# Four more on-chip buffers, and a new choice of buffer for every step, in a fused attention and gated-convolution kernel

## The chip, the cores and the metric

The kernel runs on one core of a Trainium2 chip. The core has five engines with a queue of instructions each: PE (TensorE, matrix products; its weight loads are listed apart as PEld), DVE (VectorE), ACT (ScalarE), POOL (GpSimd) and SP (SyncE, which here only issues DMA transfers). Each engine takes its own queue strictly in order; between engines, semaphores make an instruction wait. The metric is the device time of one execution in microseconds (us), the median of several runs.

## What is computed

The batch is 8, the heads 8, the sequence 576 tokens, the head size 64; channels of all heads together are 512. All is float32 (the weights come in as 64-bit floats and are narrowed on the chip).

```python
kv  = einsum('bhsd,bhse->bhde', k, v)          # 64 x 64 for each batch element and head
out = einsum('bhsd,bhde->bhse', q, kv)
x   = out / sqrt(mean(out * out, -1) + 1e-6) * g_norm   # then (B, S, H*D)
gate = sigmoid(sum_k conv_w[k] * x shifted by 4 - k tokens)   # causal, 5 taps, per channel
val  = x @ w_val                                # 512 x 512
return (gate * val) @ w_out                     # 512 x 512
```

## The kernel before

**Steps and their order.** The kernel is a list of 1,238 small steps, written out in a string `PLAN` (L19) and run one by one by the loop at L863. A step is a name, its arguments and, after an `@`, the numbers of the buffers that it takes: `fast_keep 0 3 0 @ 2` takes buffer 2 of its kind. A step puts one or a few instructions into the queue of one engine. There is no other scheduler: each engine does its steps in the order of the list. Semaphore waits are put in by the layer that records the instructions: an instruction waits for earlier instructions of the list on other engines which wrote what it reads, or which still use the buffer that it overwrites. A bank of PSUM (where PE writes its results) is treated as one buffer, also where two steps use different halves of it.

**Buffers.** `ROOMS` (L274) sets how many buffers a kind has and how large they are; `new` (L282) takes the next number off the list that the step brought along. The kinds in question are `ot` (output chunks of 128 tokens x 512 channels, 3 buffers), `gate` (3), `x` (normalised chunks of 128 tokens, 2), `sq` (squares of a chunk, 2), and the 8 banks of PSUM. `w64` (3 buffers) holds staged weights at first and sums of tokens later; `xs` (4) holds sums of x.

**One batch element, b = 0 to 7.** `load_half` and `load_q` bring k, v and q (SP). `kv_product` (PE, L475) and `kv_copy` (ACT) make kv. `turn_q` (DVE) turns q. `raw_pair` and `raw_tail` (PE, L549) make q times kv for two chunks, and the last half chunk, of 128 tokens. For each chunk, `square` (ACT, L583), `sums` (DVE, L592) and `powers` (POOL, L600) make the root, and `normalise` (ACT, L619: one instruction for each head, 8 for a chunk) writes an `x` buffer. x is then turned, for whole chunks from b = 2 on by `turn_blocks` (DVE, L644) and `move_blocks` (DMAs of SP and POOL, L652), else by `turn_x` (PE, L631) and `keep_x` (ACT, L638). The gate of one of four groups of channels is `gate_start` (ACT, L663), four `gate_tap` (DVE, L669) and `gate_end` (ACT sigmoid, L676) in a `gate` buffer; `gated` (DVE, L694) multiplies it into the values.

**The two large products.** From b = 2 on, x times w_val is made with seven products of blocks in place of eight: `x_sums` (DVE, L715) makes sums, `val_fast` (PE, L730; n = 0 to 6) the products, `val_keep` (copies by ACT, L739 to L751, and additions by DVE, L737) brings them together. The first two elements use `val_product` (PE, L681) and `keep_val` (ACT, L690). The output product is made likewise, for pairs of elements i and pairs of chunks p: `token_sums` (DVE, L799), `fast_product i p n` (PE, L821), `fast_keep i p n`. Bank a collects products n = 0, 2, 4 and 6 one after the other; another bank has b (n = 3) in its first half and c (n = 1, 5) in its second:

```python
if n == 0:   nc.scalar.copy(out=first[:, LOW], in_=a)       # L833, takes an ot buffer
elif n == 1: nc.scalar.copy(out=second[:, HIGH], in_=c)     # L835, takes an ot buffer
elif n == 2: nc.scalar.copy(out=first[:, HIGH], in_=a)      # L837
elif n == 4: add(second[:, HIGH], a)                        # L831, DVE
elif n == 5: add(first[:], both halves of b, c)             # L831, DVE
else:        copy(out=second[:, LOW], in_=a)                # L844
```

So product 2 may not be added to bank a before copy 0 has read it, and product 4 not before copy 2. `out_product` (PE, L768) and `keep_out` (ACT, L776) do the half chunks. `store` (SP, L853) writes a chunk out in four transfers; `store_last` shares the last two chunks between SP and ACT. An `ot` buffer is free for new data when the four transfers of the chunk before have landed.

Of the kernel before, what the change touches and what calls it, by code (L numbers as in the profile page):

```python
# [25 lines left out]
narrow_weight cw 0 1; sort_q 0 4; narrow_weight cw 0 2; narrow_weight cw 0 3; narrow_weight wval 1 0 @ 1;
stage_weight wout 0 @ 1; narrow_weight cw 0 4; narrow_weight wval 1 1; narrow_weight cw 0 6 @ 1;
narrow_weight cw 0 7; narrow_weight wval 1 2; turn_cw @ 1; kv_product 0 0; keep_cw; load_half v 1 0;
narrow_weight wval 1 5 @ 1; narrow_weight wval 1 3; narrow_weight wval 1 6 @ 0; start_warm 1 256 @ 1;
kv_copy 0 1; kv_copy 0 0; load_half k 1 0; narrow_weight wval 0 0 @ 0; raw_whole 0 4 @ 3;  # L30
# [5 lines left out]
narrow_weight wval 3 1; turn_q_rows 1 2 @ 6; sums 0 1; square 0 0 @ 0; powers 0 2; normalise 0 3 @ 0;
turn_q_rows 1 1 @ 7; narrow_weight wval 3 2; narrow_weight wval 3 6 @ 2; sort_q 1 2 @ 0; turn_q_rows 1 0 @ 2;
sums 0 0; sort_q 1 1; narrow_weight wval 3 3; turn_x 0 3 @ 6; narrow_weight wval 0 4; turn_q_rows 1 3 @ 7;
powers 0 1; normalise 0 4 @ 1; keep_x 0 3; normalise 0 2 @ 0; sort_q 1 4; turn_x 0 4 @ 3;
narrow_weight wval 3 4; load_q 2 0; turn_x 0 2 @ 4; keep_x 0 4; narrow_weight wval 2 5 @ 1;  # L40
kv_product 1 1 @ 6 5; narrow_weight wval 0 7; keep_x 0 2; narrow_weight wval 2 0 @ 0; val_product 0 0 1 @ 4;
narrow_weight wval 3 7; narrow_weight wval 2 1; halo 0; normalise 0 0 @ 0; narrow_weight wval 2 2;
narrow_weight wout 0 5 @ 2; normalise 0 1 @ 1; narrow_weight wval 2 3; load_q 2 2; turn_x 0 0 @ 0;
narrow_weight wout 0 6 @ 0; turn_x 0 1 @ 1; narrow_weight wval 2 4; keep_x 0 0; val_product 0 1 1 @ 3;
keep_val 0 0 1; narrow_weight wval 2 6 @ 2; keep_x 0 1; narrow_weight wval 2 7; gate_start 0 0 @ 0;
# [10 lines left out]
square 1 1 @ 0; val_product 0 2 0 @ 4; turn_q 2 2 @ 0; keep_x 1 4; gate_tap 0 3 1; powers 1 2;
normalise 1 3 @ 1; load_q 3 1; gate_tap 0 2 3; kv_product 2 1 @ 2 3; val_sums 1; square 1 0 @ 1; sums 1 1;
val_product 0 3 0 @ 7; normalise 1 2 @ 0; narrow_weight wout 1 4; powers 1 1; gate_tap 0 3 0;
stage_weight wout 3 @ 0; keep_val 0 2 0; sums 1 0; narrow_weight wout 0 3; turn_x 1 2 @ 1; turn_q 2 0;
turn_x 1 3 @ 4; powers 1 0; keep_x 1 2; kv_product 2 0; val_sums 3; keep_x 1 3; load_q 2 3; keep_val 0 3 0;  # L60
narrow_weight wout 0 4; normalise 1 1 @ 1; val_product 1 1 1 @ 4; narrow_weight wout 2 5 @ 2; halo 1;
narrow_weight wout 0 7; narrow_weight wout 1 7; gate_end 0 1; narrow_weight wout 2 6 @ 0;
val_product 1 3 1 @ 7; normalise 1 0 @ 0; turn_q 2 1; narrow_weight wout 3 5 @ 2; load_q 3 0;
narrow_weight wout 2 0 @ 0; kv_copy 2 0; keep_val 1 1 1; narrow_weight wout 3 6 @ 1; turn_x 1 0 @ 0;
narrow_weight wout 2 1; narrow_weight wout 3 0 @ 1; val_product 1 2 1 @ 4; keep_x 1 0; gate_tap 0 2 2;
narrow_weight wout 2 2; load_half v 3 0 @ 0; turn_q 2 3; load_half k 3 1 @ 0; kv_copy 2 1;
narrow_weight wout 2 3; load_half k 3 0 @ 0; gate_tap 0 2 1; turn_x 1 1 @ 3; load_q 3 2; gate_end 0 3;
raw_pair 2 3 @ 2 0; narrow_weight wout 2 4; keep_val 1 2 1; keep_x 1 1; gate_tap 0 2 0; raw_pair 2 1 @ 4 6;
square 2 2 @ 1; gated 0 1; load_half v 3 1 @ 0; gate_end 0 2; val_product 1 0 1 @ 3; gated 0 3; keep_val 1 3 1;
gate_start 1 1 @ 2; sums 2 2 @ 0 1; square 2 1 @ 0; gated 0 2; powers 2 2; square 2 0 @ 1; turn_q 3 1 @ 1;  # L70
val_product 1 0 0 @ 7; narrow_weight wout 3 1; sums 2 1; narrow_weight wout 3 2; sums 2 0; powers 2 1;
narrow_weight wout 3 3; val_product 1 3 0 @ 1; gate_tap 1 1 3; keep_val 1 0 0; narrow_weight wout 3 4;
square 2 3 @ 1; normalise 2 2 @ 1; narrow_weight wout 3 7; powers 2 0; val_product 1 1 0 @ 7; sums 2 3;
weight_sums 0; keep_val 1 0 1; normalise 2 1 @ 0; token_sums 0 0 0 @ 0; powers 2 3; val_product 1 2 0 @ 3;
turn_blocks 2 2; narrow_weight wout 2 7; normalise 2 0 @ 1; gate_tap 1 1 2; fast_product 0 1 0 @ 5;
turn_blocks 2 1; keep_val 1 3 0; weight_sums 2; keep_val 1 2 0; kv_product 3 1 @ 6 4; keep_val 1 1 0;
# [5 lines left out]
fast_product 0 0 4; move_blocks 2 1; gate_start 1 3 @ 1; sums 2 4; fast_product 0 1 2; weight_sums 3;
move_blocks 2 2; fast_keep 0 0 5; raw_pair 3 3 @ 6 4; move_blocks 2 0; fast_keep 0 1 2; fast_keep 0 0 4;
gate_tap 1 0 3; raw_pair 3 1 @ 1 7; store 0 0; square 3 2 @ 1; gated 1 1; powers 2 4; square 3 3 @ 0;
fast_product 0 0 6; gate_tap 1 3 3; gate_start 1 2 @ 2; move_blocks 2 3; sums 3 2 @ 1 0; fast_product 0 1 4;
fast_keep 0 0 6; sums 3 3; square 3 1 @ 1; fast_product 0 1 1 @ 3; gate_tap 1 0 2; normalise 2 4 @ 1;
# [811 lines left out]
```

## Time and profile before

| | |
|---|---|
| median of 3 runs | 306.62 us (306.56 to 308.01) |
| the profiled execution's own time | 308.16 us |
| its span, first to last instruction | 306.4 us |
| granted TensorE clock, mean | 0.997 |
| PE busy / DVE / ACT / POOL | 294.8 / 272.5 / 194.1 / 111.5 us |
| HBM read and written | 39.21 and 9.44 MB |

The profile is one execution. Its page lists busy time of each engine, the span in 40 slices, DMA queues, the chain of work that ended last and the costliest groups of instructions; the trace behind it answers further questions by window, tile or line. A row of a timeline gives the start, the length, the engine, the line and the operation with the tile written and the tiles read, merged where equal ones follow each other. In a list of waits, "A <- B: 5.8, 5, 1.9" means that A's engine sat idle before A for 5.8 us in total, 5 times, at most 1.9 us, until B released it. Buffer numbers are left out of the tiles' names: `bank` is any bank, `w` any `w64` buffer. [...] A DMA is told as `out_dram<-ot`, what it writes and reads.

### The profile page before, as it was taken

The numbers are of one execution on the slowest core, as the hardware profiler recorded it, in microseconds if no ns is written. First come the engines' busy times: TensorE is split into PE (matmuls) and PEld (weight loads), VectorE is DVE, ScalarE is ACT, GpSimd is POOL, SyncE is SP. The second block draws the span as 40 slices with busy tenths as digits, with TensorE's granted clock in tenths as the row PEclk, the third lists the DMA queues.
The fourth block names the chain that finished last, engine by engine and source line by source line (L and its number), as shares of the span: only waits on it lengthen the run. The fifth ranks groups of instructions, "written<-read, shape, count | busy, mean of one in ns | idle before, by whom it ended". The sixth has DMA issues, their size and how long they took to land.

```text
span 306.4 us, 8926 instructions
## 1 busy us (share of the span) xinstructions
PE 294.8 (96%) x3407; PEld 231.4 (76%) x3407; DVE 272.5 (89%) x486; ACT 194.1 (63%) x598; POOL 111.5 (36%) x127
## 2 busy tenths in 40 slices
...
GB/s 271 380 375 396 232 274 151 179 324 53 101 159 301 294 194 198 258 183 213 175 253 258 157 118 241 214 182 150 166 73 34 2 155 63 96 34 71 100 71 103
DMA packets 32074, 55.53 MB, mean 181 GB/s; under 512 B 6166, under 2 KB 14358, under 8 KB 32032
## 3 DMA queue, kind: packets, MB, share of 16 engines
...
q0 software_dynamic: 1632, 3.17, 4.4%
...
q8 instruction: 27, 0.44, 0.6%
q14 instruction: 15, 0.12, 0.1%
HBM read 39.21 MB, written 9.44 MB: 159 GB/s over the span
## 4 chain that ended last, share of the span: by engine, by line
PE 63%; DVE 11%; DMA 9%; ACT 7%; SPq 5%; issue 3%; POOL 1%; ACTq 0%; DVEq 0%; POOLq 0%
PE bank L821 24%; PE bank L730 16%; PE bank L681 7%; DMA out_dram<-ot 6%; PE bank L549 5%; PE bank L475 5%; PE bank L768 5%; SPq L853 4%; DVE gate L669 3%; DMA qs<-in_q_dram 2%; ACT x L619 2%; ACT gate L676 1%; DVE qT L532 1%; DVE ss L592 1%; PE bank L631 1%
## 5 line engine op out<-in xcount | busy, mean ns | idle before, releaser
L669 DVE SCALAR_TENSOR_TENSOR gate<-xT,cwT,gate 128x576 f32<-128x576 f32 x128 | 101.0, 807 | 1.3 <-ACT gate L663 1.0
L600 POOL TENSOR_TENSOR rt<-ss,mhalf 128x8 f32<-128x8 f32 (+3 forms) x38 | 68.6, 1816 | 68.6 <-DVE ss L592 68.3
L619 ACT ACTIVATE x<-bank,rt 128x64 f32<-128x64 f32 x252 | 55.8, 376 | 3.8 <-POOL rt L600 3.5
L652 POOL DMA_DIRECT2D xT<-y x48 | 26.7, 560 | 71.7 <-DVE w L799 25.5
L821 PE MATMUL bank<-wsum,w 128*128 128x256 f32 x192 | 49.2, 386 | 2.1 <-ACT ot L833 1.4
L821 PEld LDWEIGHTS bank<-wsum,w 128*128 128x128 f32 x192 | 35.3, 190 | 10.1 <-ACT ot L833 3.2
L730 PE MATMUL bank<-xs,vsum 128*128 128x288 f32 x144 | 38.7, 408 | 0.0
L681 PE MATMUL bank<-xT,wval 128*128 128x288 f32 x128 | 33.1, 411 | 0.0
L821 PE MATMUL bank<-wout,gv 128*128 128x256 f32 x128 | 32.6, 383 | 0.1
L730 PEld LDWEIGHTS bank<-xs,vsum 128*128 128x128 f32 x144 | 27.1, 190 | 7.4 <-issue 0.4
L681 PEld LDWEIGHTS bank<-xT,wval 128*128 128x128 f32 x128 | 23.6, 190 | 6.1
L831 DVE TENSOR_TENSOR ot<-bank,ot 128x512 f32<-128x512 f32 (+1 forms) x32 | 17.6, 551 | 11.8 <-ACT ot L837 5.7
L821 PEld LDWEIGHTS bank<-wout,gv 128*128 128x128 f32 x128 | 23.9, 190 | 4.3 <-ACT ot L835 0.5
L592 DVE TENSOR_REDUCE ss<-sq 128x8 f32<-128x520 f32 (+1 forms) x40 | 25.0, 632 | 2.2 <-ACT sq L583 2.0
L676 ACT ACTIVATE gate<-gate 128x576 f32<-128x576 f32 x32 | 22.2, 706 | 7.2 <-DVE gate L669 7.1
L730 PE MATMUL bank<-xT,wval 128*128 128x288 f32 x96 | 26.2, 408 | 0.2 <-issue 0.2
L583 ACT ACTIVATE sq<-bank 128x256 f32<-128x256 f32 (+1 forms) x70 | 21.3, 382 | 7.1 <-PE bank L549 7.0
L663 ACT ACTIVATE gate<-xT,cwT 128x576 f32<-128x576 f32 x32 | 25.1, 797 | 1.1 <-DVE gv L694 0.9
L694 DVE TENSOR_TENSOR gv<-gv,gate 128x576 f32<-128x576 f32 x32 | 23.8, 755 | 1.6 <-ACT gate L676 1.3
L730 PEld LDWEIGHTS bank<-xT,wval 128*128 128x128 f32 x96 | 17.9, 190 | 5.0 <-issue 0.3
L549 PEld LDWEIGHTS bank<-kv,qT 64*64 64x64 f32 x1008 | 16.6, 135 | 5.3 <-issue 3.7
L475 PEld LDWEIGHTS bank<-v,k 64*64 64x64 f32 x1008 | 16.4, 135 | 4.9 <-issue 2.8
...
## 6 DMA issues: line engine op xcount, KB each, us to landing
...
```

The source lines that it names most:

```text
L475: nc.tensor.matmul(st["kvps", b][s][r * D:(r + 1) * D, i], st["k", b, i][rows, r, cols], st["v", b, i][rows, r, cols], start=(j == 0), sto ...
L549: nc.tensor.matmul(st["raw", b, c][r][cols, to * D:(to + 1) * D], st["qT", b][rows, hp, first:first + D], kvs[b % 2][rows, hp, :], start=T ...
L592: nc.vector.reduce_sum(out=st["ss", b][:, FIRST[c]:FIRST[c] + n], in_=st["sq", b, c][:, 0:n], axis=AX.X)
L600: nc.gpsimd.tensor_tensor(out=st["rt", b][:, which], in0=st["ss", b][:, which], in1=mhalf[:, which], op=ALU.pow)
L619: nc.scalar.activation(out=x[:, to * D:(to + 1) * D], in_=raw[:, h * D:(h + 1) * D], func=AF.Copy, scale=root[:, to:to + 1])
L652: (nc.sync if i % 2 else nc.gpsimd).dma_start(out=xTs[b % 2][i * TB:(i + 1) * TB, :, first:first + P], in_=y[a * TB:(a + 1) * TB, i])
L663: nc.scalar.activation(out=gate[:], in_=xTs[b % 2][:, jt, HALO:SX], func=AF.Copy, scale=cwT[:, K - 1, jt:jt + 1])
L669: nc.vector.scalar_tensor_tensor(out=gate[:], in0=xTs[b % 2][:, jt, tap * TB:tap * TB + S], scalar=cwT[:, tap, jt:jt + 1], in1=gate[:], op ...
L676: nc.scalar.activation(out=gate[:], in_=gate[:], func=AF.Sigmoid)
L681: nc.tensor.matmul(val[:], wval[:, kc, jt * P:(jt + 1) * P], xTs[b % 2][:, kc, HALO + n * SV:HALO + (n + 1) * SV], start=(kc == 0), stop=( ...
L730: nc.tensor.matmul(st[bank, "val", b, mj][:], weights_[:, k], tokens()[:, k], start=(n in (0, 1, 3) and k == 0), stop=(k == NK // 2 - 1), ...
L821: nc.tensor.matmul(st[bank, i, p], tokens()[:, k], weights_[:, k], start=(n < 2 and k == 0), stop=(k == NK // 2 - 1), skip_group_check=True)
```

## The change

`ot` gets a fourth buffer, `gate` a fourth, `x` a third and `sq` a third; the number of all other buffers stays. The numbers behind the `@` are chosen anew for 474 steps: each step takes the buffer of its kind, banks included, that has been free for the longest time. The list's steps are the same 1,238. Many shift by a few places in the list, but the order on each engine, and on each queue, is the same, except that the third `sq` buffer is cleared at the start by one more memset of DVE (L324). One pair changes sides across engines: `fast_keep 2 2 1` (ACT) now stands ahead of `fast_product 2 2 3` (PE) in the list, both of which use the bank of b and c.

```diff
-    ROOMS = {"w64": (3, 1024), "ot": (3, 512), "wexp": (2, 512), "gate": (3, 576), "xs": (4, 576), "x": (2,
+    ROOMS = {"w64": (3, 1024), "ot": (4, 512), "wexp": (2, 512), "gate": (4, 576), "xs": (4, 576), "x": (3,
...
-             36), "rt": (2, 36), "sq": (2, 520)}
+             36), "rt": (2, 36), "sq": (3, 520)}
```

Of the plan, the lines that the prediction speaks of:

```diff
-keep_val 0 2 1; gate_tap 0 1 0; keep_val 0 1 0; powers 1 3; gate_start 0 2 @ 0; sums 1 2; turn_x 1 4 @ 2;
+powers 1 3; keep_val 0 1 0; gate_start 0 2 @ 3; sums 1 2; turn_x 1 4 @ 0; square 1 1 @ 0; turn_q 2 2 @ 0;
...
-val_fast 6 1 0 @ 1; powers 7 2; fast_keep 1 2 5; gate_tap 5 1 2; fast_product 1 2 6; fast_keep 1 3 0 @ 0;
+fast_keep 1 3 0 @ 3; powers 7 2; val_fast 6 1 0 @ 0; fast_keep 1 2 5; gate_tap 5 1 2; store 1 4;
...
-fast_product 2 2 4; gate_start 6 0 @ 0; gate_tap 6 3 1; fast_keep 2 3 0 @ 1; fast_product 2 2 3;
-gate_tap 6 0 3; move_blocks 7 2; fast_keep 2 2 1 @ 0; token_sums 2 1 3; fast_product 2 3 2; powers 7 4;
+fast_keep 2 2 1 @ 1; gate_tap 6 0 3; move_blocks 7 2; fast_product 2 2 3; token_sums 2 1 3; fast_product 2 3 2;
```

More of the change, by code (lines that the diff above doesn't have):

```diff
@@ L26 @@
[L26 to L30, printed above, removed]
@@ L36 @@
[L36 to L40, printed above, removed]
@@ L41 @@
[L41 to L45, printed above, removed]
@@ L56 @@
[L56 to L60, printed above, removed]
@@ L61 @@
[L61 to L76, printed above, removed]
@@ L82 @@
[L82 to L86, printed above, removed]
@@ L87 @@
-powers 3 3; load_half v 4 0 @ 0; fast_product 0 1 3; gate_tap 1 2 3; square 3 0 @ 0; gate_tap 1 0 1;
-turn_x 2 4 @ 0; load_half k 4 1 @ 0; val_fast 2 0 3 @ 2; load_q 4 0; fast_keep 0 1 1 @ 1; powers 3 2; sums 3 0;
-normalise 3 3 @ 1; fast_product 0 1 5; fast_keep 0 1 4; gate_tap 1 2 2; fast_product 0 1 6; gate_tap 1 3 2;
-keep_x 2 4; load_q 4 1; powers 3 0; normalise 3 2 @ 0; val_fast 2 0 0 @ 0; fast_keep 0 1 5; x_sums 2 0 @ 0;
-val_fast 2 1 0 @ 3; fast_keep 0 1 6; sums 3 1; halo 2; val_keep 2 0 0; val_fast 2 0 1 @ 5; x_sums 2 1 @ 1;
@@ L107 @@
-fast_product 0 3 1 @ 6; gate_tap 2 1 2; normalise 3 4 @ 1; fast_product 0 2 5; sums 4 2 @ 1 1; gate_end 2 3;
-gate_tap 2 1 1; fast_product 0 2 6; powers 4 2; fast_keep 0 2 5; turn_x 3 4 @ 2; load_q 5 0;
-raw_pair 4 1 @ 0 7; fast_keep 0 2 6; sums 4 3; keep_x 3 4; gated 2 3; val_fast 3 0 0 @ 2; powers 4 3;
-square 4 0 @ 0; gate_tap 2 1 0; val_fast 3 0 3 @ 1; sums 4 0; val_keep 3 0 0; square 4 1 @ 1; x_sums 3 0 @ 0;
-load_half v 5 1 @ 0; halo 3; val_fast 3 1 0 @ 5; store 0 4; val_keep 3 0 3; x_sums 3 2 @ 1; val_fast 3 1 3 @ 1;
@@ L147 @@
-gated 3 1; powers 5 4; move_blocks 5 3; fast_product 1 1 6; val_keep 4 0 6; gate_tap 4 0 1;
-out_product 1 8 @ 5; val_keep 4 1 3; normalise 5 4 @ 1; gate_tap 4 3 1; gate_start 4 2 @ 2; gate_tap 4 0 0;
-kv_copy 6 0; gate_tap 4 3 0; turn_q 6 0 @ 1; gate_end 4 3; gate_tap 4 2 3; turn_x 5 4 @ 0; load_q 6 3;
-val_fast 5 1 0 @ 4; keep_x 5 4; gated 4 3; halo 5; val_fast 5 0 0 @ 0; x_sums 5 0 @ 3; gate_start 4 1 @ 0;
-turn_q 6 2; load_half k 7 1 @ 0; fast_keep 1 1 6; val_fast 5 1 1 @ 6; load_half v 7 1 @ 0; val_keep 5 0 0;
@@ L177 @@
-fast_product 1 2 4; gate_tap 5 1 3; square 7 2 @ 0; sums 7 3 @ 1 0; val_fast 6 0 0 @ 3; keep_x 6 4;
-fast_keep 1 2 1 @ 2; gate_tap 5 3 0; fast_product 1 2 5; sums 7 2; val_keep 6 0 0; fast_keep 1 2 4;
-val_fast 6 1 0 @ 1; powers 7 2; fast_keep 1 2 5; gate_tap 5 1 2; fast_product 1 2 6; fast_keep 1 3 0 @ 0;
-store 1 4; val_keep 6 1 0; gate_end 5 3; x_sums 6 0 @ 3; val_fast 6 1 3 @ 2; powers 7 3; normalise 7 2 @ 1;
-x_sums 6 1 @ 0; fast_product 1 3 2; gated 5 3; val_fast 6 0 2; gate_tap 5 1 1; fast_keep 1 3 2; halo 6;
@@ L197 @@
-move_blocks 7 0; val_keep 6 0 5; fast_product 2 2 5; gate_tap 6 2 2; fast_keep 2 3 2; gate_tap 6 0 2;
-fast_product 2 3 4; normalise 7 4 @ 1; gate_tap 6 2 1; val_fast 6 0 6; gate_tap 6 2 0; turn_x 7 4 @ 4;
-fast_product 2 3 1 @ 6; val_keep 6 0 6; gate_tap 6 3 0; keep_x 7 4; fast_product 2 3 3; halo 7;
-fast_keep 2 2 4; gate_tap 6 0 1; fast_product 2 2 6; gate_tap 6 0 0; val_fast 7 0 0 @ 4; x_sums 7 0 @ 1;
-gate_end 6 0; fast_keep 2 2 5; val_fast 7 1 0 @ 3; fast_keep 2 2 6; gate_end 6 2; x_sums 7 1 @ 3; store 2 4;
@@ L222 @@
-fast_keep 3 2 2; fast_keep 3 2 5; fast_product 3 2 4; store 3 4; fast_product 3 3 0 @ 0; fast_keep 3 2 4;
-fast_product 3 2 6; fast_keep 3 3 0 @ 1; fast_product 3 3 2; fast_product 3 3 3; fast_keep 3 3 2;
-fast_keep 3 2 6; fast_product 3 3 4; store 3 5; fast_keep 3 3 1 @ 2; fast_product 3 3 5; fast_keep 3 3 4;
+stage_weight cw 0 @ 0; turn_q_rows 0 4 @ 1; turn_q_rows 0 2 @ 2; turn_q_rows 0 1 @ 3; turn_q_rows 0 3 @ 4;
+sort_q 0 1 @ 0; turn_q_rows 0 0 @ 5; start_warm 3 256 @ 6; sort_q 0 0; load_q_rows 1 0; stage_weight wval 3;
@@ new lines @@
+turn_x 0 4 @ 4; load_q 2 0; turn_x 0 2 @ 6; narrow_weight wval 2 5 @ 0; keep_x 0 4; kv_product 1 1 @ 7 3;
+narrow_weight wval 0 7; keep_x 0 2; narrow_weight wval 2 0 @ 0; narrow_weight wval 3 7; narrow_weight wval 2 1;
+val_product 0 0 1 @ 4; halo 0; normalise 0 0 @ 0; narrow_weight wval 2 2; load_q 2 2;
+narrow_weight wout 0 5 @ 2; normalise 0 1 @ 1; narrow_weight wval 2 3; narrow_weight wout 0 6 @ 1;
+turn_x 0 0 @ 6; turn_x 0 1 @ 5; narrow_weight wval 2 4; keep_x 0 0; val_product 0 1 1 @ 1;
+narrow_weight wval 2 6 @ 3; keep_val 0 0 1; keep_x 0 1; narrow_weight wval 2 7; gate_start 0 0 @ 0;
@@ new lines @@
+val_product 0 2 0 @ 1; keep_x 1 4; powers 1 2; normalise 1 3 @ 0; gate_tap 0 3 1; load_q 3 1; gate_tap 0 2 3;
+kv_product 2 1 @ 6 3; val_sums 1; square 1 0 @ 2; sums 1 1; normalise 1 2 @ 1; val_product 0 3 0 @ 0;
+narrow_weight wout 1 4; powers 1 1; gate_tap 0 3 0; stage_weight wout 3 @ 2; keep_val 0 2 0;
+narrow_weight wout 0 3; sums 1 0; turn_x 1 2 @ 5; turn_q 2 0; powers 1 0; turn_x 1 3 @ 7; keep_x 1 2;
+kv_product 2 0; val_sums 3; load_q 2 3; keep_x 1 3; narrow_weight wout 0 4; keep_val 0 3 0; normalise 1 1 @ 2;
@@ new lines @@
+val_product 1 1 1 @ 1; narrow_weight wout 2 5 @ 3; halo 1; narrow_weight wout 0 7; narrow_weight wout 1 7;
+gate_end 0 1; narrow_weight wout 2 6 @ 2; normalise 1 0 @ 1; val_product 1 3 1 @ 5; turn_q 2 1;
+narrow_weight wout 3 5 @ 1; load_q 3 0; narrow_weight wout 2 0 @ 1; kv_copy 2 0; narrow_weight wout 3 6 @ 0;
+keep_val 1 1 1; narrow_weight wout 2 1; turn_x 1 0 @ 7; narrow_weight wout 3 0 @ 0; val_product 1 2 1 @ 0;
+gate_tap 0 2 2; keep_x 1 0; load_half v 3 0 @ 0; narrow_weight wout 2 2; turn_q 2 3; load_half k 3 1 @ 0;
@@ new lines @@
+kv_copy 2 1; load_half k 3 0 @ 0; narrow_weight wout 2 3; gate_tap 0 2 1; load_q 3 2; turn_x 1 1 @ 2;
+gate_end 0 3; narrow_weight wout 2 4; raw_pair 2 3 @ 6 4; keep_val 1 2 1; gate_tap 0 2 0; keep_x 1 1;
+raw_pair 2 1 @ 1 7; gated 0 1; square 2 2 @ 1; load_half v 3 1 @ 0; gate_end 0 2; gated 0 3;
+val_product 1 0 1 @ 3; keep_val 1 3 1; sums 2 2 @ 0 0; gate_start 1 1 @ 0; gated 0 2; square 2 1 @ 0;
+powers 2 2; square 2 0 @ 2; turn_q 3 1 @ 1; val_product 1 0 0 @ 0; narrow_weight wout 3 1; sums 2 1;
@@ new lines @@
+kv_product 3 1 @ 7 1; keep_val 1 1 0; turn_q 3 0; turn_q 3 2; load_q 3 3; fast_product 0 0 1 @ 2;
+gate_tap 1 1 1; fast_product 0 0 3; token_sums 0 0 1; fast_keep 0 0 1 @ 3; normalise 2 3 @ 0;
+token_sums 0 0 2 @ 0; fast_product 0 0 0 @ 0; weight_sums 1; kv_product 3 0; gate_tap 1 1 0;
+fast_keep 0 0 0 @ 1; gate_start 1 0 @ 2; token_sums 0 0 3; raw_tail 2 @ 4 5; kv_copy 3 1; fast_product 0 0 2;
+kv_copy 3 0; turn_blocks 2 3; gate_end 1 1; turn_blocks 2 0; fast_product 0 0 5; fast_keep 0 0 2; turn_q 3 3;
@@ new lines @@
+fast_keep 0 1 0 @ 0; move_blocks 2 1; square 2 4 @ 0; fast_product 0 0 4; gate_start 1 3 @ 1; sums 2 4;
+move_blocks 2 2; weight_sums 3; fast_product 0 1 2; fast_keep 0 0 5; move_blocks 2 0; raw_pair 3 3 @ 6 1;
+fast_keep 0 0 4; fast_keep 0 1 2; gate_tap 1 0 3; store 0 0; raw_pair 3 1 @ 2 7; powers 2 4; gated 1 1;
+square 3 2 @ 2; square 3 3 @ 1; gate_tap 1 3 3; fast_product 0 0 6; gate_start 1 2 @ 3; move_blocks 2 3;
+sums 3 2 @ 1 1; fast_product 0 1 4; sums 3 3; fast_keep 0 0 6; square 3 1 @ 0; gate_tap 1 0 2;
@@ new lines @@
+fast_product 0 1 1 @ 0; powers 3 3; normalise 2 4 @ 1; load_half v 4 0 @ 0; gate_tap 1 2 3; fast_product 0 1 3;
+square 3 0 @ 2; load_half k 4 1 @ 0; gate_tap 1 0 1; fast_keep 0 1 1 @ 2; turn_x 2 4 @ 4; load_q 4 0;
+val_fast 2 0 3 @ 5; powers 3 2; normalise 3 3 @ 0; sums 3 0; fast_keep 0 1 4; fast_product 0 1 5;
+gate_tap 1 2 2; keep_x 2 4; load_q 4 1; fast_product 0 1 6; gate_tap 1 3 2; powers 3 0; normalise 3 2 @ 2;
+fast_keep 0 1 5; val_fast 2 0 0 @ 4; x_sums 2 0 @ 0; fast_keep 0 1 6; val_fast 2 1 0 @ 0; sums 3 1; halo 2;
@@ new lines @@
+square 4 3 @ 2; fast_keep 0 2 4; gate_tap 2 1 2; square 4 2 @ 0; fast_product 0 3 1 @ 2; normalise 3 4 @ 0;
+sums 4 2 @ 0 0; fast_product 0 2 5; gate_end 2 3; gate_tap 2 1 1; powers 4 2; load_q 5 1; fast_product 0 2 6;
+fast_keep 0 2 5; sums 4 3; turn_x 3 4 @ 0; fast_keep 0 2 6; raw_pair 4 1 @ 6 1; keep_x 3 4; gated 2 3;
+powers 4 3; gate_tap 2 1 0; square 4 0 @ 1; load_q 5 0; sums 4 0; val_fast 3 0 0 @ 7; val_fast 3 0 3 @ 3;
+val_keep 3 0 0; square 4 1 @ 0; val_fast 3 1 0 @ 0; x_sums 3 0 @ 0; halo 3; load_half v 5 1 @ 0;
@@ new lines @@
+val_keep 3 0 3; val_keep 3 1 0; store 0 4; x_sums 3 2 @ 2; val_fast 3 1 3 @ 3; normalise 4 2 @ 1;
+x_sums 3 1 @ 1; powers 4 0; fast_product 0 3 3; gate_tap 2 0 2; normalise 4 3 @ 2; val_fast 3 0 2;
+val_keep 3 1 3; load_q 5 2; sums 4 1; val_fast 3 0 1 @ 3; gate_tap 2 0 1; powers 4 1; gate_tap 2 0 0;
+val_fast 3 1 2; turn_blocks 4 3; gate_end 2 0; val_fast 3 1 1 @ 4; x_sums 3 3 @ 3; val_keep 3 0 1;
+gate_start 2 2 @ 1; val_fast 3 0 5; gated 2 0; val_keep 3 1 1; store 0 5; val_keep 3 0 2; gate_tap 2 2 3;
@@ new lines @@
+fast_keep 0 3 6; fast_keep 0 3 5; raw_pair 5 3 @ 3 1; store 0 7; fast_keep 1 0 2; powers 4 4; gate_tap 3 0 3;
+raw_pair 5 1 @ 7 5; token_sums 1 0 3 @ 1; square 5 3 @ 1; move_blocks 4 0; gate_tap 3 0 2; normalise 4 4 @ 1;
+fast_product 1 1 1 @ 2; sums 5 3 @ 1 1; square 5 0 @ 0; move_blocks 4 1; fast_product 1 0 1 @ 0;
+gate_tap 3 3 1; square 5 2 @ 2; powers 5 3; token_sums 1 0 2; fast_product 1 0 3; fast_keep 1 0 1 @ 1;
+gate_tap 3 3 0; fast_product 1 0 4; load_q 6 1; sums 5 2; gate_end 3 3; turn_x 4 4 @ 6; gate_tap 3 1 3;
@@ new lines @@
+fast_product 1 1 3; powers 5 2; keep_x 4 4; normalise 5 3 @ 0; fast_keep 1 0 4; fast_product 1 0 5; sums 5 0;
+load_q 6 2; gate_tap 3 0 1; fast_product 1 0 6; powers 5 0; normalise 5 2 @ 2; fast_keep 1 0 5;
+val_fast 4 0 0 @ 6; x_sums 4 0 @ 1; halo 4; load_half k 6 1 @ 0; x_sums 4 2 @ 0; val_fast 4 1 0 @ 0;
+val_keep 4 0 0; x_sums 4 1 @ 2; square 5 1 @ 1; val_fast 4 1 1 @ 1; gated 3 3; sums 5 1; val_fast 4 0 2;
+val_keep 4 1 1; turn_blocks 5 3; val_keep 4 1 0; powers 5 1; fast_keep 1 0 6; val_fast 4 0 1 @ 3;
@@ new lines @@
+val_keep 4 1 5; gated 3 0; kv_product 6 1 @ 3 1; x_sums 4 3 @ 3; fast_keep 1 1 0 @ 1; load_q 6 0;
+gate_start 4 3 @ 2; gated 3 2; gate_start 4 0 @ 3; fast_product 1 1 2; turn_blocks 5 0; turn_blocks 5 1;
+val_fast 4 1 4; gate_tap 4 0 3; raw_tail 5 @ 5 7; kv_product 6 0; val_keep 4 1 4; square 5 4 @ 2;
+gate_tap 3 1 0; val_fast 4 1 6; sums 5 4; move_blocks 5 0; kv_copy 6 1; gate_end 3 1; gate_tap 4 3 3;
+fast_keep 1 1 2; move_blocks 5 2; val_fast 4 1 3 @ 1; gate_tap 4 3 2; val_keep 4 1 6; val_keep 4 0 4;
@@ new lines @@
+move_blocks 5 1; fast_product 1 1 4; gate_tap 4 0 2; val_fast 4 0 6; fast_keep 1 1 4; powers 5 4;
+move_blocks 5 3; gated 3 1; fast_product 1 1 6; val_keep 4 0 6; gate_tap 4 0 1; normalise 5 4 @ 2;
+out_product 1 8 @ 0; val_keep 4 1 3; gate_tap 4 3 1; gate_start 4 2 @ 1; gate_tap 4 0 0; kv_copy 6 0;
+gate_tap 4 3 0; turn_q 6 0 @ 0; gate_end 4 3; gate_tap 4 2 3; load_q 6 3; turn_x 5 4 @ 6; val_fast 5 1 0 @ 1;
+keep_x 5 4; gated 4 3; gate_start 4 1 @ 0; halo 5; x_sums 5 0 @ 1; val_fast 5 0 0 @ 5; fast_keep 1 1 6;
@@ new lines @@
+token_sums 1 1 0 @ 1; kv_product 7 1 @ 6 4; fast_keep 2 1 2; fast_keep 2 0 4; normalise 6 0 @ 2;
+turn_blocks 6 3; fast_product 2 1 4; fast_keep 2 0 5; token_sums 1 1 1; store 2 0; normalise 6 1 @ 0;
+fast_product 1 3 1 @ 2; gate_tap 5 3 3; fast_product 2 0 6; gate_tap 5 3 2; load_q 7 3; kv_product 7 0;
+gate_tap 5 2 2; token_sums 1 1 3 @ 2; raw_tail 6 @ 0 3; kv_copy 7 0; fast_product 1 3 3; gate_tap 5 2 1;
+kv_copy 7 1; fast_keep 2 0 6; fast_keep 2 1 1 @ 1; store 2 1; gate_start 5 0 @ 0; turn_blocks 6 0;
@@ new lines @@
+raw_pair 7 3 @ 7 1; gate_tap 5 3 1; gate_start 5 1 @ 3; turn_x 6 4 @ 0; square 7 3 @ 1; gate_tap 5 1 3;
+fast_product 1 2 4; store 2 3; square 7 2 @ 0; sums 7 3 @ 1 1; keep_x 6 4; fast_keep 1 2 1 @ 0;
+val_fast 6 0 0 @ 3; gate_tap 5 3 0; sums 7 2; fast_product 1 2 5; val_keep 6 0 0; fast_keep 1 2 4;
+fast_keep 1 3 0 @ 3; powers 7 2; val_fast 6 1 0 @ 0; fast_keep 1 2 5; gate_tap 5 1 2; store 1 4;
+fast_product 1 2 6; val_keep 6 1 0; gate_end 5 3; x_sums 6 0 @ 1; powers 7 3; val_fast 6 1 3 @ 4;
+normalise 7 2 @ 2; x_sums 6 1 @ 2; fast_product 1 3 2; gated 5 3; halo 6; gate_tap 5 1 1; val_fast 6 0 2;
```

251 lines of the change are left out of this document (121 added, 130 removed).

## The prediction

> **What bounds the kernel now.** I read the page's busy times first, then busy time by stage, then the waits, then timelines around the longest of them. Busy times, and three stages of the span (length, then busy us of PE, PEld, DVE, ACT, POOL):
>
> ```profile
> PE 294.8 (96%) x3407; PEld 231.4 (76%) x3407; DVE 272.5 (89%) x486; ACT 194.1 (63%) x598; POOL 111.5 (36%) x127
> ```
>
> ```profile
> 20.00:137.00 117.00, 115.96 (x1627) 92.91 (x1627) 114.78 (x201) 93.66 (x296) 58.17 (x54) 1.00 0.76 223
> 137.00:290.00 153.00, 150.76 (x1463) 116.26 (x1463) 145.39 (x240) 88.05 (x273) 50.93 (x64) 1.00 0.52 139
> 290.00:306.40 16.40, 11.46 (x52) 9.36 (x50) 2.66 (x5) 2.90 (x8) 0.00 (x0) 0.93 0.31 83
> ```
>
> PE is nearly full in all stages and alone from 290 on, so what PE loses before its last product is what the end loses. DVE stands close behind: it lacks 2.2 us of 117 in the first stage and 7.6 of 153 in the second. Next, the waits of the tile `ot` (idle time of the waiting engine in us, times), and the list of all waits (us, times, longest):
>
> ```profile
> its engine sat idle before it (us, times) until:
>   PE bank L821: 35.7, 27
>   DMA out_dram<-ot: 10.9, 10
> ```
>
> ```profile
> ACT ot L835 <- DMA out_dram<-ot: 5.8, 5, 1.9
> ACT ot L833 <- DMA out_dram<-ot: 4.8, 4, 3.4
> ...
> PEld bank L821 <- ACT ot L833: 3.2, 5, 0.9
> ```
>
> ACT waits 10.6 us for stores to land, because a copy into `ot` needs a buffer whose last store is through. ACT has 112 us of idle time, so these 10.6 are no gain by themselves. They count where PE waits for ACT: `fast_product` n=2 adds to bank a, which `fast_keep` n=0 (L833) must have copied first. The longest such place, in order of time (start, length, engine, line; in brackets the idle time before it):
>
> ```profile
> 223.62 1.03 PE L821 MATMUL bank<-wsum,gv 128*128 128x256 f32 x4
> ...
> 224.48 1.13 PE L730 MATMUL bank<-xT,wval 128*128 128x288 f32 x4
> ...
> 225.59 0.37 ACT L833 COPY ot<-bank 128x256 f32<-128x256 f32 x1 [3.37 <-DMA out_dram<-ot]
> ...
> 226.02 1.13 PE L821 MATMUL bank<-wsum,w 128*128 128x256 f32 x4 [0.40 <-ACT ot L833]
> ...
> 228.30 0.44 ACT L837 COPY ot<-bank 128x256 f32<-128x256 f32 x1
> ...
> 228.79 0.92 PE L821 MATMUL bank<-wsum,w 128*128 128x256 f32 x3 [0.68 <-ACT ot L837]
> ```
>
> Matmul ends are modelled, so I count starts. An unhindered group of four L821 takes 0.86 us to the next start (223.62 to 224.48), four L730 take 0.97 (chain of waits). PE is thus free at 225.45 and starts at 226.02: 0.57 lost. The group after a stop takes 0.96 (226.02 to 226.98, the next row of PE), 0.10 more. At 228.79 another 0.84 is lost, to an ACT that is late by the same wait.
>
> **The change part by part.** *Same order.* The instructions of each engine's queue, SP's and POOL's among them, stand as before; only which buffer a step takes changes, and with it the waits. Added is one memset of DVE (a row of 65 ns) in DVE's idle 1.72 to 8.87: nothing.
>
> *Fourth `ot`.* For each of the 36 chunks I set its first copy against the landing of the last store from the buffer that the new plan gives it. Examples: the copy at 151.86 waited for a landing at 151.79, the new buffer's landed at 138.29; at 163.91 163.63 becomes 151.79; at 197.44 197.26 becomes 170.41; at 225.59 225.49 becomes 221.16, where ACT gets there at 222.22. All ten waits go; the thinnest margin is that last one, 1.06 us, the others have 2.5 or more. Where PE stopped for such a copy, and what is late next:
> - 167.38: L475 from 165.83 needs 1.21, so 0.34 lost. L833 there starts 0.7 earlier (the sigmoid behind the freed copy then waits for DVE's tap, 0.78 us of room).
> - 197.86: group from 196.43, 0.57 lost; the copy then starts at ACT's own pace, 196.84.
> - 215.63: 0.15. 221.68: 0.06. 226.02: 0.57. 228.79: 0.84. 268.01 (PE free at 267.77): 0.24.
>
> Together 2.77 us, and 0.10 for the slower group at four of them (167, 197, 226, 228): 3.17. The stops at 203.63 and 292.16 stay: there ACT waits for PE and PE for ACT, no store between.
>
> *Does DVE give way?* PE's gain is only kept if what DVE makes comes earlier too. Nearest uses: `x_sums` 0.28 us ahead of PE at 181.71, 0.34 at 184.62, 0.15 at 263.17. DVE's idle times that hang on late ACT or PE are 0.36 (152), 0.46 (174), 1.23 (201), 0.18 (211), 0.96 (219), 1.07 (226.88, the sigmoid behind the 3.37 wait), 0.27 (233) and 0.46 (237): 4.99 in all, of which those that follow PE shrink only as PE gains. At 181.71 DVE has 0.8 in hand against PE's 0.4, by 263 about 3: enough, with nothing over.
>
> *Fourth `gate`.* ACT L663 waits for DVE L694 twice, 0.9 us; no PE stop lies behind either: zero. *Third `x`, third `sq`.* No row has ACT waiting for the readers of x or sq: zero.
>
> *Banks.* At 47.50 `turn_x 1 4` waited for `keep_val` to empty its bank; the new bank is free. The chunk itself is ready at 46.86, PE at 46.5, so 0.64 to 1.0 us goes. But the next uses are near: 0.12 us of room behind ACT at 74.92, 0.05 behind `keep_x` at 92.95, 0.24 behind DVE at 125.01, and at 137.53 a load of k that landed 0.14 before its use, issued from SP behind a chain of DVE work. DVE idles only 2.2 us in this stage. Bounds 0 and 1.0 of gain; I take 0, by the row at 137.53 that it meets last. Against this, new bank waits appear: 0.16 and 0.11 us late by the old times at 80.01 and 156.25 (the first was paid one instruction later before), and this one:
>
> ```profile
> 250.01 1.03 PE L821 MATMUL bank<-wout,gv 128*128 128x256 f32 x4
> ...
> 251.08 0.37 ACT L835 COPY ot<-bank 128x256 f32<-128x256 f32 x1 [1.20 <-PE bank L821]
> ```
>
> `fast_product 2 2 3` writes half b of a bank whose half c `fast_keep 2 2 1` (L835) copies. The plan now has the copy first. So ACT no longer waits 1.20, and PE must wait: L833 ends at 249.88, then the copy to 250.25, PE at 250.30 rather than 250.01: 0.29 and 0.10, a loss of 0.4 us. Queued behind it is all of PE.
>
> The Trainium skill ("PSUM — Partial Sum Buffer", "PSUM bank collisions raise a hardware error") says that two engines may not touch one bank and quadrant at once, even at different columns, and to guard by bank. The trace agrees: L835's release is a matmul that writes the other half. By that rule the gain is 2.77; were halves guarded apart it would be 3.17, or 303.4 us.
>
> **Sum:** 3.17 - 0.40 = 2.77, say 2.8 us. The profiled execution took 308.16 us (span 306.4), 1.5 above the median of the runs, 306.62; the stops are of the program's order, so I take them off both: 305.4 for such an execution, **303.8 us** for the median. The tail behind the last product is unchanged.
>
> **Rivals.**
> - *A, DVE is the bound.* If its idle times don't close, PE meets `x_sums` at 181.71 and 263.17 with 0.28 and 0.15 us of gain left: 0.4 at most, 306.2 us. For: 97% busy from 20 to 290. Against: six of the eight idle times name ACT, and ACT comes earlier. 0.15.
> - *B, the 3.37 wait stays in part*, since the 1.06 margin is the thinnest and stores move with the work. Then 0.57 + 0.84 + 0.20 stay lost: 305.4. Against: ACT gets there earlier only by what PE gained, and so does the store. 0.12.
> - *C, the gain at 47.50 is carried to the end* since ACT's freed waits (0.84 at 90.61) pull DVE and the load along: 303.8 - 0.75 (between its 0.64 and 1.0) = 303.0. Against: the margins above. 0.14.
> - *D, slower:* the bank shared by halves at 250. PE now stands behind L837, L663, L833 and L835 of ACT; each us that ACT is late there is a us of PE. With one set of eight L619 ahead (1.75 us) and no more gain than A's, 306.62 - 0.4 + 0.4 + 1.75 = 308.4. It decides once ACT is over 1.74 us late, since ACT sits idle so long before L837 at 248.49. Against: the order is unchanged, and ACT comes early. 0.06.
>
> The forecast, 303.3 to 304.6, has 0.53. That the change doesn't remove the waits it names is B's case, read from the landings.
>
> **Range.** Below: the whole 1.0 at 47.50 and no loss at 250, 302.4. Above: A with the two small new waits, 306.5. Some 0.5%, 1.5 us, is what a measurement tells from no change, so faster means below 305.1: forecast, C and a third of B, 0.71; same 0.23 (A, the rest of B); slower 0.06 (D).
>
> **What would show it.** Right: the waits of `ot` for its stores near zero; no PE stop before the n=2 and n=4 products near 167, 197, 226 and 229; DVE's wait for the sigmoid of 1.07 gone; a new PE stop of some 0.3 us at product 2 2 3 and L835's wait of 1.20 gone; PE busy with the same work in a span near 303.6. Wrong: `ot` rows still released by stores (B), PE waits for DVE L715 or L737 that were not there (A), loads of k or v ending PE's waits, or a long stop at product 2 2 3 (D).

## The result, and the profile after

The changed kernel takes 303.19 us (median of 4 runs, 302.77 to 304.0), the kernel before 306.78 beside it: a ratio of 0.9878 (95% interval 0.9844 to 0.9912), 3.6 us faster. Forecast were 303.8 us and 2.8 us. The profiled execution took 302.96 us with a span of 301.1, near its median; that of before (308.16) lay above its own, so the two spans differ by more, 5.3 us, than the medians.

Busy times of the changed kernel by the page, then by stage as before (length, then PE, PEld, DVE, ACT, POOL):

```profile
PE 291.6 (97%) x3407; PEld 230.1 (76%) x3407; DVE 272.2 (90%) x487; ACT 193.4 (64%) x598; POOL 114.6 (38%) x127
```

```profile
19.00:135.00 116.00, 115.47 (x1624) 92.48 (x1624) 114.04 (x200) 93.33 (x296) 58.52 (x54) 1.00 0.77 228
135.00:285.00 150.00, 149.67 (x1466) 116.87 (x1465) 145.61 (x241) 87.50 (x274) 53.67 (x64) 1.00 0.53 143
285.00:301.10 16.10, 11.25 (x51) 9.18 (x50) 2.66 (x5) 2.90 (x8) 0.00 (x0) 1.00 0.32 83
```

The work is the same: DVE is busy for 145.6 us in the middle stage, 145.4 before. The stage is 3 us shorter around it. Where the waits went, by the tile `ot`:

```profile
its engine sat idle before it (us, times) until:
  PE bank L821: 39.5, 31
  DMA out_dram<-ot: 5.7, 1
```

Ten waits for stores, 10.9 us, have become one line of 5.7. Nine of the ten were copies of ACT (10.6 us); the tenth was 0.38 us before an addition of DVE at 301.10. The line of 5.7 is no copy either: it is DVE's idle time before its first addition after 289 us, also 5.70 us long before and then put down to ACT L837. No copy of ACT waits for a store any more. The place where the longest such wait stood:

```profile
219.00 0.38 ACT L833 COPY ot<-bank 128x256 f32<-128x256 f32 x1
...
221.20 1.13 PE L730 MATMUL bank<-xT,wval 128*128 128x288 f32 x4
...
222.17 1.03 PE L821 MATMUL bank<-wsum,w 128*128 128x256 f32 x4
...
223.03 1.14 PE L730 MATMUL bank<-xs,vsum 128*128 128x288 f32 x4
223.23 0.37 ACT L837 COPY ot<-bank 128x256 f32<-128x256 f32 x1
...
224.00 0.81 PE L821 MATMUL bank<-wsum,w 128*128 128x256 f32 x3
```

The copy L833 now ends over 2 us ahead of the matmul that needs it. PE goes from group to group in 0.97, 0.86 and 0.97 us, which is its unhindered pace (a group of L821, `x4`, is one `fast_product`: two matmuls of the program, each of which the trace lists as two rows, 448 in all for 224); before, 1.54, 0.96 and 1.81 stood there. The waits of PE itself that are left (us, times, longest) hold two copies, the last two stops of this kind:

```profile
PE bank L821 <- ACT ot L835: 0.5, 1, 0.5
...
PE bank L821 <- ACT ot L833: 0.3, 1, 0.3
```

### The profile page after: what moved, and what is told of

Same layout as the page of the kernel before. It is cut to its first block, busy times and chain, and to the rows that moved or that the text cites. A ratio compares the mean times of both kernels' runs of the same rounds, so it can differ in the third digit from the quotient of the medians.

```text
span 301.1 us, 8910 instructions
## 1 busy us (share of the span) xinstructions
PE 291.6 (97%) x3407; PEld 230.1 (76%) x3407; DVE 272.2 (90%) x487; ACT 193.4 (64%) x598; POOL 114.6 (38%) x127
## 4 chain that ended last, share of the span: by engine, by line
PE 77%; DVE 8%; DMA 7%; ACT 3%; issue 1%; SPq 1%; POOL 1%
PE bank L821 31%; PE bank L730 26%; DMA k<-in_k_dram 6%; PE bank L681 5%; PE bank L549 5%; PE bank L768 5%; PE bank L475 5%; DVE gate L669 2%; ACT x L619 2%; PE bank L631 1%; DVE ss L592 1%; DVE x L609 1%; POOL rt L600 1%; DMA qs<-in_q_dram 1%; DVE ot L421 1%
## 5 line engine op out<-in xcount | busy, mean ns | idle before, releaser
L600 POOL TENSOR_TENSOR rt<-ss,mhalf 128x8 f32<-128x8 f32 (+3 forms) x38 | 69.3, 1833 | 62.0 <-DVE ss L592 61.7
L821 PE MATMUL bank<-wsum,w 128*128 128x256 f32 x192 | 48.8, 384 | 0.3 <-ACT ot L833 0.3
L821 PEld LDWEIGHTS bank<-wsum,w 128*128 128x128 f32 x192 | 35.5, 190 | 7.2 <-DVE w L799 0.8
L821 PE MATMUL bank<-wout,gv 128*128 128x256 f32 x128 | 32.6, 383 | 0.0
L821 PEld LDWEIGHTS bank<-wout,gv 128*128 128x128 f32 x128 | 23.9, 190 | 4.2 <-ACT ot L835 0.3
L475 PEld LDWEIGHTS bank<-v,k 64*64 64x64 f32 x1008 | 16.0, 135 | 3.9 <-issue 2.8
## 6 DMA issues: line engine op xcount, KB each, us to landing
w<-in_moe_w_out_dram SPq DMA_DIRECT2D x4, 512.0 KB, 10.6
```

Of the source, the lines that this page charges most:

```text
L475: nc.tensor.matmul(st["kvps", b][s][r * D:(r + 1) * D, i], st["k", b, i][rows, r, cols], st["v", b, i][rows, r, cols], start=(j == 0), sto ...
L600: nc.gpsimd.tensor_tensor(out=st["rt", b][:, which], in0=st["ss", b][:, which], in1=mhalf[:, which], op=ALU.pow)
L821: nc.tensor.matmul(st[bank, i, p], tokens()[:, k], weights_[:, k], start=(n < 2 and k == 0), stop=(k == NK // 2 - 1), skip_group_check=True)
```

## The experiments

Each was timed against the kernel before, which took 307.13 us beside runs 1 to 4, 307.12 beside runs 6, 7, 8 and 10, and 307.43 beside runs 5, 9 and 11. Ratios are to before, with 95% intervals.

**1. The fourth `ot` alone** (before, with `ot` as changed):

```diff
-    ROOMS = {"w64": (3, 1024), "ot": (3, 512),
+    ROOMS = {"w64": (3, 1024), "ot": (4, 512),
...
-fast_keep 1 3 0 @ 0
+fast_keep 1 3 0 @ 3
```

> The kernel before with one thing changed: the fourth ot buffer, with the changed kernel's numbers for ot. Theory (PE's stops behind late copies into ot are the gain): no copy waits for a store, PE's stops near 167, 197, 215, 226, 229 and 268 us go, 3.2 us less than before (306.8 to 303.6). Rival (banks and the other buffers carry it, or DVE would hold PE back without them): less than 1.0 us faster, 305.8 or more.

Measured: 303.84 us, 0.9892 (0.9871 to 0.9912), 3.3 us faster. Its trace has one line of waits for stores, and that is the addition of DVE again:

```profile
  DMA out_dram<-ot: 5.7, 1
```

The stops at 167 to 229 and 268 us are gone; the one of 1.0 us at 47 and those of 0.49 and 0.62 near 202 and 288 stay. So this part alone makes almost the whole gain.

**2. Everything but the fourth `ot`** (changed, with three buffers and the old numbers for `ot`):

```diff
-    ROOMS = {"w64": (3, 1024), "ot": (4, 512),
+    ROOMS = {"w64": (3, 1024), "ot": (3, 512),
```

> The changed kernel with three ot buffers and the old numbers for ot, all else as changed. Theory: the waits for stores are back (some 10 us of ACT), and only the early gain of about 0.6 us that the two traces show by 137 us stays: 306.2. Rival (banks and other buffers carry it): 304 or less.

Measured: 307.36 us, 1.0008 (0.9987 to 1.003): no gain that can be told, 0.4 us at most by the interval, and 1.2 us above what was expected. The early 0.6 us does not show in the median. By the trace the waits for stores are back, with PE's stops of 0.89 and 0.84 us near 224 and 227:

```profile
  DMA out_dram<-ot: 12.2, 7
```

The rival falls with both runs: banks and the other buffers don't carry the gain.

**3. Product 2 2 3 ahead of keep 2 2 1 again** (changed):

```diff
-fast_keep 2 2 1 @ 1; gate_tap 6 0 3; move_blocks 7 2; fast_product 2 2 3;
+fast_product 2 2 3; fast_keep 2 2 1 @ 1; gate_tap 6 0 3; move_blocks 7 2;
```

> The changed kernel with fast_product 2 2 3 put back ahead of fast_keep 2 2 1 in the list. Theory: PE's stop there (0.11 us and 0.10 for the slower group, by the trace of the changed kernel) goes and ACT waits for the product again, 1.2 us, with nothing of PE's behind it: 0.2 us less, 303.0. Rival (the early copy is worth something to ACT or DVE): 303.2 or more.

Measured: 303.28 us, 0.9883 (0.9859 to 0.9908), against 0.9878. A size of 0.2 us is too small to tell in the time: inconclusive. The trace has what the theory says: PE's groups there follow in 0.86 us each, without a stop, and L835 waits 1.28 us for the product.

**4. One wait for a store put back** (changed, with the `ot` numbers 1 and 3 exchanged from here on, in ten steps, so that this copy waits for the last store again):

```diff
-fast_keep 1 3 0 @ 3
+fast_keep 1 3 0 @ 1
```

> The changed kernel with the ot numbers 1 and 3 exchanged from fast_keep 1 3 0 on: this copy gets the buffer whose store lands last, as it had before, and fast_keep 1 3 1 the one that it gets now. Theory: one wait of some 3 us returns before the copy near 219 us, and with it PE's two stops of 0.57 and 0.84 and two slower groups: 1.6 us more, 304.8. Rival (such a wait is hidden, or DVE sets the pace there anyway): under 0.5 us more.

Measured: 305.59 us, 0.9948 (0.9928 to 0.9967), 2.4 us above the changed kernel and 0.8 above what was expected. Its trace has the whole chain back:

```profile
221.50 1.13 PE L730 MATMUL bank<-xT,wval 128*128 128x288 f32 x4
223.26 1.13 PE L821 MATMUL bank<-wsum,w 128*128 128x256 f32 x4 [0.62 <-ACT ot L833]
224.23 1.13 PE L730 MATMUL bank<-xs,vsum 128*128 128x288 f32 x4
226.04 0.70 PE L821 MATMUL bank<-wsum,w 128*128 128x256 f32 x2 [0.69 <-ACT ot L837]
```

```profile
222.83 0.37 ACT L833 COPY ot<-bank 128x256 f32<-128x256 f32 x1 [3.43 <-DMA out_dram<-ot]
```

PE is free at 222.47 (221.50 and 0.97) and at 225.20, so 0.79 and 0.84 us are lost, and with two slower groups 1.8. The other 0.6 us of the medians' distance lies inside the two intervals. One wait of 3.4 us on ACT, before one of 36 first copies, is half of the gain by the trace and two thirds by the medians.

**5. The wait at 47.50 alone** (before):

```diff
-turn_x 1 4 @ 2
+turn_x 1 4 @ 7
```

> The kernel before with one bank number changed: turn_x 1 4 takes bank 7 in place of 2, so it no longer waits for keep_val. Theory: PE's stop of 1.0 us at 47.50 goes but is lost again by 80 to 137 us, since DVE and loads come no earlier: within 0.3 us of 307.1. Rival (carried to the end): 0.6 to 1.0 us less, 306.3.

Measured: 307.18 us, 0.9981 (0.9953 to 1.0009): no difference that can be told. The stop at 47 shrank from 1.0 to 0.41 us. Of the 0.60 us won there 0.27 was left by 60 us, and the profiled execution then lost 1.7 us near 117, to another cause (last section).

**6. The new banks alone** (before, with the changed kernel's numbers for banks, in 137 steps; in all the number behind the `@` differs in 291 steps, not in 474, of the 417 that take a buffer):

> The kernel before with the changed kernel's numbers for the banks alone. Theory (late copies into ot are nearly all of it): the stop at 47.50 goes and the early products start some 0.4 us earlier, but most of it is lost again by 80 us, and the ot waits stay: 0 to 0.6 us less than before, so 306.5 to 307.1. Rival (the gain at 47.50 is carried to the end): 1.0 us less or more.

Measured: 306.55 us, 0.9981 (0.996 to 1.0001). As the theory has it, though a gain of 0.6 us and none both lie in the interval. The profiled execution took 309.61 us, 3 us above the median.

**7. Fourth gate, third x, third sq alone** (before):

```diff
-"gate": (3, 576), "xs": (4, 576), "x": (2,
+"gate": (4, 576), "xs": (4, 576), "x": (3,
...
-             36), "rt": (2, 36), "sq": (2, 520)}
+             36), "rt": (2, 36), "sq": (3, 520)}
```

> The kernel before with the fourth gate, the third x and the third sq, in the changed kernel's numbers for these three. Theory: no stop of PE stands behind a wait for them: no difference, within 0.3 us of 307.1. Rival (ACT's two waits before gate_start, 0.9 us, reach DVE and PE): 0.5 to 1 us less.

Measured: 306.87 us, 0.999 (0.9974 to 1.0007): nothing that can be told.

**8 and 9. Less work for DVE**, in the changed kernel and in the one before (16 steps dropped from the plan, `gate_tap b jt 0` for b = 3 to 6):

> The changed kernel with the last of the four taps (tap 0) left out for batch elements 3 to 6: 16 of DVE's instructions of 0.81 us, 13 us of DVE's work, so its output lacks a part of the gate. Theory (PE sets the pace, DVE keeps up with nothing over): under 1 us less, 302.4 to 303.2. Rival (DVE is the bound now): 3 us less or more, 300 or less.

> The kernel before with tap 0 left out for batch elements 3 to 6 (13 us of DVE's work; the output lacks a part of the gate). Theory (the stops behind late copies into ot were PE's, not DVE's): under 1 us less, 306.2 to 307.1. Rival (DVE's load set the pace before): 2 us less or more.

Measured: 303.38 us, 0.9876 (0.9856 to 0.9895), and 307.97 us, 1.0011 (0.9983 to 1.0039); the first is 0.2 us, the second 0.9 us above what was expected. The page of the first shows that the work is gone, 11 us of it:

```profile
PE 291.6 (97%) x3407; PEld 229.8 (76%) x3407; DVE 261.1 (86%) x471; ACT 193.1 (64%) x598; POOL 112.4 (37%) x127
```

Neither kernel got faster, so both rivals fall. DVE, busy for 95 to 98% of the first two stages, was the bound of neither.

**10. The last two stops** (changed, three steps moved):

```diff
-token_sums 2 0 2; normalise 6 3 @ 1;
+token_sums 2 0 2; fast_keep 2 1 0 @ 3; normalise 6 3 @ 1;
...
-fast_product 3 2 3; fast_keep 3 2 1 @ 0; keep_out 3 8 @ 3;
-fast_product 3 2 5; fast_keep 3 2 0 @ 1; store 3 8; fast_product 3 2 2;
+fast_product 3 2 3; fast_keep 3 2 0 @ 1; fast_keep 3 2 1 @ 0; keep_out 3 8 @ 3;
+fast_product 3 2 2; fast_product 3 2 5; store 3 8;
```

> The changed kernel with two of PE's last stops taken on: fast_keep 2 1 0 goes ahead of normalise 6 3 on ACT (the stop of 0.49 us at 200.77), and near the end fast_keep 3 2 0 ahead of fast_keep 3 2 1 and fast_product 3 2 2 ahead of fast_product 3 2 5 (the stop of 0.62 us at 286.95, which then has a product of 0.86 us beside it). Theory (each stop of PE is time of the end): 1.1 us and 0.2 for the slower groups less, 301.9. Rival (DVE or ACT would hold PE back in its place): under 0.4 us less, 302.8 or more.

Measured: 302.17 us, 0.9835 (0.9815 to 0.9855), with the next one the fastest of all, 1.0 us below the changed kernel. The two intervals overlap slightly, but no execution of one lies in the range of the other (301.75 to 302.6, and 302.77 to 304.0), and by the traces PE gains 0.59 and 0.72 us at the two places, 1.3 as expected. Where the stop of 0.62 us stood, the groups now follow in 0.87, 0.86 and 0.86 us (the first row a group's first part):

```profile
285.29 1.03 PE L821 MATMUL bank<-wout,gv 128*128 128x256 f32 x4
286.16 1.03 PE L821 MATMUL bank<-wsum,w 128*128 128x256 f32 x4
287.02 1.03 PE L821 MATMUL bank<-wout,w 128*128 128x256 f32 x4
287.88 0.38 PE L821 MATMUL bank<-wsum,w 128*128 128x256 f32 x1
```

The copy that was moved ahead, L833 at 283.55, now does wait for a store, 3.14 us. It costs nothing: PE was busy with L768 until 284.33.

**11. A fifth `ot`** (10, with the third `x` given back, and `ot` always the one free longest):

```diff
-"ot": (4, 512), "wexp": (2, 512), "gate": (4, 576), "xs": (4, 576), "x": (3,
+"ot": (5, 512), "wexp": (2, 512), "gate": (4, 576), "xs": (4, 576), "x": (2,
```

> The kernel with the two stops mended (302.2 us), with a fifth ot buffer, and the third x given back (2, with the old numbers), since there is no room for both. Theory (with four, no copy waits for a store any more, and the third x carries nothing): the same, 302.2 within 0.3. Rival (some waits for stores are left in other executions than the profiled one, or x matters): 0.5 us less or more.

Measured: 302.42 us, 0.9833 (0.9793 to 0.9874): no difference from run 10 that can be told, so a fifth buffer shows no gain. Two things change at once here, so a small gain of one could hide a small loss of the other; that the third `x` carries nothing rests on run 7 as well.

## Why the prediction was right, point by point

A measure for each step is PE's lead: the start of one matmul before, less its start after, in the two profiles. By it, from 167 us on:

| place (us, before) | forecast gain | measured gain |
|---|---|---|
| 167.38 | 0.44 | 0.34 |
| 169.86 | 0 | 0.20 |
| 197.86 | 0.67 | 0.67 |
| 215.63 and 221.68 | 0.21 | 0.42 |
| 226.02 | 0.67 | 0.67 |
| 228.79 | 0.94 | 0.95 |
| 250.01 | -0.39 | -0.21 |
| 263.17 | 0 | 0.17 |
| 268.01 | 0.24 | 0.35 |
| sum | 2.78 | 3.56 |

- *The fourth `ot`, and that PE's stops are what counts:* right, step by step, and shown by runs 1, 2 and 4. The trace of run 1 has the same gains at the same places, but for 250.01, where it has none. At 215, 221 and 268 the stops were taken 0.1 too small each: the group behind the stop is the slower one there too, and the forecast had added 0.10 us at four of the seven only. At 167 it had added it wrongly: that group, behind L475, takes 0.97 us in the changed kernel too.
- *Waits that were read as room:* at 263.17 the prediction gave `x_sums` 0.15 us of room ahead of PE. But PE was waiting. From the matmul before to this one it took 0.34 us, where 0.24 is its pace, and DVE's row ends at 263.03, just before PE loads the weights:

```profile
262.27 0.76 DVE L715 TENSOR_TENSOR xs<-xT 128x576 f32<-128x576 f32 x1
...
263.14 0.54 PEld L730 LDWEIGHTS bank<-xs,vsum 128*128 128x128 f32 x3 [0.36 <-issue]
```

  After, DVE ends 0.51 us ahead of the same matmul and the stop is gone. The same holds at 92.95, where "0.05 behind `keep_x`" was a wait for it: 0.28 us are won from 91 to 94, 0.27 of it in run 1 too, behind the copy that had waited 0.84 us at 90.61. At 169.86 the prediction did not see that PE waits 0.2 us for a load of k (landed at 169.73).
- *Product 2 2 3 behind keep 2 2 1:* the mechanism was right, the size too large:

```profile
244.25 1.03 PE L821 MATMUL bank<-wsum,w 128*128 128x256 f32 x4
244.53 0.36 ACT L833 COPY ot<-bank 128x256 f32<-128x256 f32 x1
244.78 0.38 ACT L835 COPY ot<-bank 128x256 f32<-128x256 f32 x1
245.22 0.73 PEld L821 LDWEIGHTS bank<-wout,gv 128*128 128x128 f32 x4 [0.35 <-ACT ot L835]
245.22 1.13 PE L821 MATMUL bank<-wout,gv 128*128 128x256 f32 x4
```

  PE was free at 245.11 and lost 0.11 and 0.10. The forecast had let L835 start where L833 ends; it starts 0.25 after L833's start, 0.11 ahead of its end, as one copy of ACT overlaps the next. Rival D (a long stop here) fell. The Trainium skill ("PSUM — Partial Sum Buffer", "PSUM bank collisions raise a hardware error") says to guard PSUM by bank and quadrant, or simply by bank. The program does the latter, and the trace shows what it costs here. No run here shows what unguarded halves would do.
- *The early stop at 47.50, taken as nothing:* nearly right in size, but not for the reason given. The lead goes from 1.24 to 2.09 us there and is back at 1.40 by 53.2, so 0.16 is kept. What takes the rest is neither DVE nor the load at 137.53: the next `turn_x` meets ACT's `normalise` at once:

```profile
51.61 0.77 PE L631 MATMUL bank<-ident,x 128*128 128x128 f32 x5 [0.28 <-ACT x L619]
```

  Run 5, which removes this wait alone, gained nothing that can be told. Rival C fell. Of the two new bank waits foretold, the one at 80.01 came and was made good by 80.3, and the one at 156.25 did not come; 0.19 us are lost near 149 instead, to a bank that `normalise` still reads.
- *Rival A, DVE:* fell, by runs 8 and 9 most plainly. The forecast was right that DVE would keep up, but "nothing over" was too cautious.
- *Rival B, the thin margin of 1.06 us:* did not come about; run 4 shows what it would have cost.
- *What the sum left out at the start:* the lead already stands at 1.24 us by 17.7. Some 0.5 us is the late start of that one execution of before: runs 1, 5, 7 and 9, with the old banks, have 0.27 to 0.55 there as well. The rest comes with the new banks, whose eight profiles have 0.85 to 1.48. With the old banks a `kv_product` stops some 0.37 us near 10 us for DVE L532 to empty its bank; with the new ones it does not, but that gain is lost again by 15.66, where PE waits longer for ACT L404. What stays is in the next `kv_product`: from its first start to the next step's it takes 1.21 to 1.65 us with the new banks and 1.97 to 2.31 with the old ones. The profile puts the stop inside it down to nothing ("issue"), and its cause is open. The forecast did not price it. How much of it reaches the end is not settled: run 6 has 0.6 us with an interval that touches none, run 2 has no gain, and run 1 lacks 0.65 of the changed kernel's gain, inside the intervals as well.

The gain was 3.6 us where 2.8 was forecast, and the table's two sums differ by as much: 0.37 by waits taken for room or not seen, 0.22 by slower groups, 0.18 by the overlap on ACT. That the profiles' 3.56 meets the medians' 3.6 so closely is partly luck: by its interval the gain lies between 2.7 and 4.8 us, and the early lead is not in the table.

## What to carry to other kernels

Where one engine is nearly full, count its stops by the starts of its instructions and ask of each which buffer stands at the end of the chain. Nine waits of another engine, 10.6 us in all, were worth 3.3 us, since only six of them had PE behind them, and one wait alone held half of it. Set each first use of a buffer against the landing of the last transfer out of it: that table told which waits would go. A start 0.05 to 0.15 us behind what it needs, and further from the start before it than the pace, is a wait and no room. And a second engine's busy share, even over 95%, does not make it a bound: taking 11 us of its work away moved nothing that could be told.

## What had not been expected

Waits for stores are not the same in every execution. In run 5, one that does not show in the profile of before stopped PE for most of two microseconds (ACT, then PE, near 117 us):

```profile
117.34 0.37 ACT L835 COPY ot<-bank 128x256 f32<-128x256 f32 x1 [4.38 <-DMA out_dram<-ot]
```

```profile
114.98 1.16 PE L549 MATMUL bank<-kv,qT 64*64 64x64 f32 x64
117.76 1.13 PE L821 MATMUL bank<-wout,gv 128*128 128x256 f32 x4 [1.62 <-ACT ot L835]
```

At the same place the copy in before waited for PE (2.14 us) and for no store. Runs 2, 6, 7 and 9 have the wait for a store here, 2.3 to 3.4 us; only in run 6 did it stop PE, for 0.7 us. With three buffers the executions of before, beside run 1, lay between 305.49 and 308.73 us (22 of them); with four, those of run 1 between 303.21 and 304.57 (6). So some of the scatter may come in by these waits, though so few runs don't settle it. Some comes in by loads; in run 11 a load of k stopped PE:

```profile
167.47 0.47 PE L549 MATMUL bank<-kv,qT 64*64 64x64 f32 x16
169.75 0.94 PE L475 MATMUL bank<-v,k 64*64 64x64 f32 x49 [1.81 <-DMA k<-in_k_dram]
```

In the changed kernel the same product started 0.28 us behind the one before it, with no stop. It is the product at 169.86 of before; runs 5 and 7 waited 0.5 and 1.0 us there for this load.
